# Loading, the first block and the last denominators of an attention kernel rearranged

## The chip, the cores and the metric

The kernel runs on one core of a Trainium2 chip. The metric is the device time of one execution in microseconds (us); where several runs are shown, their median counts. A core has five engines that each work off their own list of instructions in order: TensorE (PE in the profile; its weight loads are PEld), VectorE (DVE), ScalarE (ACT), GpSimd (POOL) and SyncE (SP), which here issues nearly all transfers. Engines wait for each other by semaphores.

## The reference

A layer norm of `x` (2048 x 512, bf16) feeds two branches, which are added to `x`:

```
xn  = layernorm(x)
qkv = xn @ wqkv                       # 32 heads of 16
p   = softmax(q k^T / 4)              # 2048 x 2048 for each head
A   = (p v) @ wo
h   = layernorm(xn)
B   = (gelu(h^T w1 + b1) w2 + b2)^T   # mixes tokens: w1 is 2048x1376
out = x + A + B
```

The exponentials, 32 x 2048 x 2048 of them, are the bulk of the elementwise work.

## The kernel before, in words

**Tiling.** The 2048 tokens are 16 tiles of 128. The attention runs over 32 blocks: for each of four blocks of 512 queries, eight sets of four heads, of which the four live in 32-row strips of TensorE. A block has 16 groups, one for each tile of 128 keys, so there are 512 groups. The scores of a group are four matmuls of 32 x 128 by 512 queries (`score_mm`, L553).

**Two ways to the exponential.** A group goes either to ScalarE, as two exponentials of 128 x 1024 from a pair of PSUM banks (`exp_tile`, L561; banks 0 and 1, or 2 and 3), or to VectorE, which builds it from integer arithmetic on the bits of bf16: four instructions from PSUM (L607) and two further "planes" in SBUF (L612). The products with V (L573) are added up in bank 6 (`PV_BANK`). V has a 17th column of ones for each head, so row 16 of each strip of bank 6 holds the denominator of the softmax. A second copy of V, `V17b`, is scaled by 0.75 for the third plane. The columns of zeros and ones between the heads are written by `v_consts`.

**Order.** The program is written out by a planner in Python. `sc.add` appends an instruction to an engine's list and gives it a planned start from `occ` (how long it holds the engine) and `lat` (until its result can be read); `dma` does the same for transfers. These durations decide only the order. The beginning is an order by hand: loads, constants, statistics and normalization of the first four tiles (`ln_stats1`, `ln_stats2`, `ln_norm`), their transposes (`transpose_mm`) and evacuations (`xnT_evac`), K of the first four tiles and the first 512 queries (`k_mm`, `qt0_mm`, `k_evac`, `qt_evac`). `zeros(n)` puts n matmuls with zero weights on TensorE in between. From there a dispatcher takes engine by engine: it places scores for the next free pair of banks, fills TensorE with products, projections and the MLP's matmuls as far as they end within `TOL` of the next scores, hands groups to VectorE when that has little left to do, and adds a zero matmul (L1524) where TensorE had fewer than `KEEP` units of work in the last 3.4 us. Tiles 4 to 15 go through the chains `ln1` (statistics, normalization), `tp` (transpose) and `kv` (K and V for the first four heads) while block 0 is already running.

**The end.** In each block but the last the denominators travel through DRAM to be inverted and spread. In the last one, `tail_epilogue`, VectorE spreads row 16 of each strip over 32 rows by a shuffle of 128 x 256 (two halves), ScalarE forms exp(-ln(d)), and VectorE multiplies; then come a matmul with the second half of the last rows of `wo` for each of four output tiles (`op_half`, L906), the addition of the rest (`fin`, L1702) and the store.

Of the kernel before, what the change touches and what calls it, by code (L numbers as in the profile page):

```python
# [8 lines left out]
ACTF = mybir.ActivationFunctionType  # L9
# [248 lines left out]
def bass_parallel_sum__softmax_full_mha__mixer_token_mlp__prompt_kernel(  # L258
# [18 lines left out]
    with ExitStack() as es:  # L277
# [67 lines left out]
        def dma(q, dst, src, reads, writes, name="", noncontig=False, out_dma=False, lat=2500.0, move=150.0):  # L345
# [4 lines left out]
            else:  # L350
                def fn(eng, dst=dst, src=src):
# [9 lines left out]

        sc.add("pool", lambda e: e.memset(ident[:], 0.0), writes=[("ident",)], occ=300)
        sc.add("pool", lambda e: e.affine_select(ident[:], ident[:], [[-1, 128]], ALU.not_equal, 1.0,
                                                 base=0, channel_multiplier=1),
               reads=[("ident",)], writes=[("ident",)], occ=600)
        sc.add("pool", lambda e: e.memset(mhalf[:], -0.5), writes=[("mhalf",)], occ=200)
        v17_views = []
# [16 lines left out]
        sc.add("pool", lambda e: e.memset(qmask[:, 0:1], 0.0), writes=[("qmask",)], occ=200)  # L384
        for r in range(4):
            sc.add("pool", lambda e, r=r: e.memset(qmask[32 * r:32 * r + 16, 0:1], QSCALE),
                   reads=[("qmask",)], writes=[("qmask",)], occ=200)
        sc.add("pool", lambda e: e.tensor_scalar(qmask[:, 1:2], qmask[:, 0:1], -1.0, QSCALE, ALU.mult, ALU.add),
               reads=[("qmask",)], writes=[("qmask",)], occ=250)

# [118 lines left out]

        def qt_evac(qb, T, e_, bk, eng="dve"):  # L510
            slot = (8 * qb + 2 * T + e_) % NQS
            if eng == "act":
                return sc.add("act", lambda e: e.activation(QT[:, slot, :], bank(bk), ACTF.Identity,
                                                            scale=qmask[:, e_:e_ + 1]),
                              reads=[("bank", bk), ("qmask",)], writes=[("QT", slot)], occ=560, lat=740)
            return sc.add("dve", lambda e: e.tensor_scalar(QT[:, slot, :], bank(bk), qmask[:, e_:e_ + 1], None,
                                                           ALU.mult),
                          reads=[("bank", bk), ("qmask",)], writes=[("QT", slot)], occ=650, lat=790)

# [30 lines left out]
        def score_mm(g, r, bk, last):  # L550
            b, kt, qb, G, T, e_ = blk_of(g)
            slot_q = b % NQS
            return sc.add("pe", lambda e: e.matmul(  # L553
                bank(bk), lhsT=KT[32 * r:32 * r + 32, T, 128 * kt:128 * (kt + 1)],
                rhs=QT[32 * r:32 * r + 32, slot_q, :], start=True, stop=True,
                tile_position=(32 * r, 0)),
                reads=[("KTt", T, kt), ("QT", slot_q), ("QTr", slot_q, r)], writes=[("bank", bk)], name="sc",
                occ=(222.0 if last else 4.0), lat=430.0, cfg="S")
# [94 lines left out]
        def xnT_evac(t, n, bk, half, eng):  # L653
            dst = xnT[:, t // 4, :, 128 * (t % 4):128 * (t % 4 + n)].rearrange("p c (n j) -> p n c j", n=n)
            src = ps_bf[:, bk * 1024 + half * 512: bk * 1024 + (half + n) * 512].rearrange(
                "p (n c j) -> p n c j", n=n, c=NCT)
            if n == 1:
                dst, src = dst[:, 0], src[:, 0]
            return evac(eng, dst, src, reads=[("bank", bk)], writes=[("xnT", t + i) for i in range(n)], n=256 * n)

# [39 lines left out]
        qt_evac(0, 0, 1, QB, "dve")  # L700
        v_consts(0, "pool")


# [274 lines left out]
        def chain_ln1(t, due):  # L978
            def fin():
                op = ln_norm(t)  # L980
                ln1_done.add(t)
                return op
            return Chain("ln1.%d" % t, [Step("dve", lambda: ln_stats1(t), 755),
                                        Step("pool", lambda: ln_stats2(t), 820),
                                        Step("dve", fin, 300, two=True)], due, 0.0)

# [377 lines left out]
        def pv_candidates(t):  # L1364
            b = pv_block[0]
            if b >= NBLK or not pv_open[0]:
                return []
            return [it for it in pv_items[b] if it[0] <= t and (b > 0 or it[2] % NKT in (v0_done if it[1] == "A" else v0b_done))]

# [20 lines left out]

        TOL = 120.0
        JOIN = 45.0
# [65 lines left out]
        def pe_step(t):  # L1458
# [78 lines left out]

        KEEP = 8.0
        n_zero = [0]

# [129 lines left out]
        def tail_epilogue():  # L1670
            b = NBLK - 1
            po = par_o(b)

            sc.add("act", lambda e: e.activation(u_sb[:, 0:1], r2[:, 0:1], ACTF.Ln), reads=[("r2",)], writes=[("u",)],
                   occ=2800)
            HC = 256
            halves = [slice(HC * i, HC * (i + 1)) for i in range(2)]

            def spread(i):
                sc.add("dve", lambda e: e.stream_shuffle(denb[:, halves[i]], bank(PV_BANK)[:, halves[i]], [16] * 32),  # L1680
                       reads=[("bank", PV_BANK)], writes=[("denb", r) for r in range(4)] if i == 0 else [("denc", 1)],
                       occ=360, lat=490)

            def invert(i):
                key = ("denb", 0) if i == 0 else ("denc", 1)
                for f, sl in ((ACTF.Ln, 1.0), (ACTF.Exp, -1.0)):
                    sc.add("act", lambda e, f=f, sl=sl: e.activation(denb[:, halves[i]], denb[:, halves[i]], f, scale=sl),  # L1687
                           reads=[key], writes=[key], occ=64 + HC / 1.2, lat=242 + HC / 1.2)

            def mult(i):  # L1690
                key = ("denb", 0) if i == 0 else ("denc", 1)
                sc.add("dve", lambda e: e.tensor_tensor(otmp[:, po, halves[i]], bank(PV_BANK)[:, halves[i]],
                                                        denb[:, halves[i]], ALU.mult),
                       reads=[("bank", PV_BANK), key], writes=[("otmp", po, 2 * i), ("otmp", po, 2 * i + 1)],
                       **T_DVE(HC))
                for c in (2 * i, 2 * i + 1):
                    op_half(1, 1, c, c, False, True)
# [102 lines left out]
```

## Time and profile before

| | us |
|---|---|
| median of three runs | 709.04 (708.06 to 709.98) |
| the profiled execution | 710.63 |
| its span, first to last instruction | 708.8 |
| ScalarE busy | 690.5 (97%) |
| VectorE busy | 666.1 (94%) |
| TensorE busy | 655.9 (93%) |
| GpSimd busy | 62.9 (9%) |
| first exponential of ScalarE starts | 11.42 |
| last exponential of ScalarE starts | 694.1 |

A line of a group or of the timeline reads: line of the kernel, engine, operation, what is written from what, shapes and count. In the list of groups the busy time follows and the mean of one in ns, then the idle time of the engine just ahead of them and what ended it. In the timeline the first two numbers are the start and the length in us. In tables by stretch the first number is the stretch's length, and each engine's busy time has its count of instructions behind it. A busy TensorE is not TensorE at its peak: each matmul of 512 columns is recorded with some 0.39 us, while a row of them starts one every 0.22.

### The profile page before, as it was taken

How to read it: one execution, taken by the hardware profiler on the slowest of the kernel's cores; microseconds unless marked ns; L12 is line 12 of the kernel's file. 1: busy time of each engine (PE TensorE's matmuls, PEld its weight loads, DVE VectorE, ACT ScalarE, POOL GpSimd, SP SyncE). 2: the span in 40 equal slices, each digit the busy share in tenths (PEclk: the TensorE clock that was granted, in tenths of full speed). 3: DMA queues.
4: the chain of work that ended last, by engine and by line, in shares of the span. 5: the costliest groups of instructions: out<-in, count | busy, mean ns of one | idle time of the engine just before them, and what ended most of it. 6: DMA issues, size and time to landing. Idle time of an engine off the chain costs nothing.

```text
span 708.8 us, 15538 instructions
## 1 busy us (share of the span) xinstructions
PE 655.9 (93%) x6146; PEld 201.3 (28%) x6235; DVE 666.1 (94%) x1152; ACT 690.5 (97%) x760; POOL 62.9 (9%) x91
## 2 busy tenths in 40 slices
PE   8999999999999999999999999998999999898984
PEld 4533333222222222222222222222222222222221
DVE  6889999999999999999999999999999999999994
ACT  5899999999999999999999999999999999999996
POOL 6420100000000000000000000000000000000000
PEclk9899999999999999999999999999999999999998
DMA  7015110122230312002221212211211111111000
GB/s 208 1 47 101 34 27 4 27 47 55 53 73 15 75 46 53 17 20 54 59 56 47 68 38 48 52 44 44 56 45 38 40 35 54 25 30 31 17 30 30
DMA packets 78368, 32.66 MB, mean 46 GB/s; under 512 B 63004, under 2 KB 74204, under 8 KB 78296
## 3 DMA queue, kind: packets, MB, share of 16 engines
q1 hardware_dynamic: 77240, 31.40, 18.3%
q8 instruction: 49, 0.80, 0.5%
q10 hardware_dynamic: 1056, 0.26, 0.2%
q14 instruction: 23, 0.19, 0.1%
HBM read 26.08 MB, written 2.61 MB: 40 GB/s over the span
## 4 chain that ended last, share of the span: by engine, by line
ACT 88%; PE 8%; DVE 3%; issue 1%; DMA 0%; DVEq 0%; ACTq 0%; SPq 0%
ACT pT L561 86%; PE ps L553 3%; PE ps L573 3%; PE ps L493 1%; DVE x_sb L607 1%; ACT ga_sb L872 1%; PE ps L626 1%; ACT L1687 1%; PE ps L888 0%; DMA x_sb<-in_A_x_dram 0%; PE ps L898 0%; DVE plx L607 0%; DVE stats L442 0%; DVE x_sb L612 0%; DVE xn_sb L612 0%
## 5 line engine op out<-in xcount | busy, mean ns | idle before, releaser
L561 ACT ACTIVATE pT<-ps 128x1024 bf16<-128x1024 f32 x734 | 676.3, 1131 | 4.8 <-PE ps L553 4.6
L553 PE MATMUL ps<-QT,KT 32*128 32x512 bf16 x2048 | 291.7, 385 | 28.6 <-ACT pT L561 23.7
L607 DVE TENSOR_SCALAR x_sb<-ps 128x512 int16<-128x512 f32 x404 | 274.9, 685 | 14.2 <-PE ps L553 1.2
L553 PEld LDWEIGHTS ps<-QT,KT 32*128 32x128 bf16 x2048 | 74.3, 91 | 284.6 <-ACT pT L561 271.6
L573 PE MATMUL ps<-pT,V 128*32 128x512 bf16 x1468 | 146.1, 392 | 2.4 <-DVE V L489 0.8
L607 DVE TENSOR_SCALAR plx<-ps 128x512 int16<-128x512 f32 x148 | 98.4, 682 | 1.3 <-PE ps L553 0.8
L612 DVE TENSOR_SCALAR x_sb<-x_sb 128x2048 int16<-128x2048 int16 x135 | 92.8, 693 | 3.3 <-PE ps L573 2.7
L573 PE MATMUL ps<-x_sb,V 128*32 128x512 bf16 x812 | 77.0, 382 | 1.3 <-DVE x_sb L612 1.0
L573 PEld LDWEIGHTS ps<-pT,V 128*32 128x32 bf16 x1468 | 37.3, 93 | 83.8 <-issue 74.5
L888 PE MATMUL ps<-gT,w2blk 128*128 128x512 bf16 (+1 forms) x148 | 49.3, 385 | 3.0 <-issue 2.5
L851 PE MATMUL ps<-h_sb,w1blk 128*128 128x512 bf16 (+1 forms) x154 | 48.7, 385 | 2.1 <-issue 1.9
L1104 POOL TENSOR_TENSOR oT<-OT,denb 128x512 bf16<-128x512 f32 x16 | 20.4, 1272 | 324.6 <-DVE x_sb L612 175.8
L1104 POOL TENSOR_TENSOR otmp<-OT,denb 128x512 bf16<-128x512 f32 x15 | 19.1, 1272 | 280.9 <-DVE x_sb L612 155.3
L612 DVE TENSOR_SCALAR x_sb<-plx 128x2048 int16<-128x2048 int16 x62 | 42.1, 685 | 0.2
L573 PE MATMUL ps<-x_sb,V17b 128*32 128x512 bf16 x416 | 40.8, 382 | 0.2 <-DVE x_sb L612 0.2
L493 PE MATMUL ps<-xnT,wqkv_sb 128*128 128x512 bf16 (+1 forms) x166 | 35.0, 309 | 3.3 <-issue 2.6
L612 DVE TENSOR_SCALAR plx<-x_sb 128x2048 int16<-128x2048 int16 x48 | 33.1, 689 | 1.0 <-PE ps L573 0.5
L573 PE MATMUL ps<-plx,V 128*32 128x512 bf16 x284 | 27.7, 381 | 0.7 <-DVE OT L1067 0.6
L573 PEld LDWEIGHTS ps<-x_sb,V 128*32 128x32 bf16 x812 | 21.8, 96 | 16.1 <-issue 7.5
L1067 DVE COPY OT<-ps 128x512 f32<-128x512 f32 x31 | 21.1, 680 | 0.1
L493 PE MATMUL ps<-wqkv_sb,xnT 128*128 128x128 bf16 x256 | 21.1, 223 | 0.0
L888 PEld LDWEIGHTS ps<-gT,w2blk 128*128 128x128 bf16 (+1 forms) x176 | 12.8, 97 | 26.9 <-issue 22.9
(88 smaller groups left out, 358.6 us busy)
## 6 DMA issues: line engine op xcount, KB each, us to landing
denb<-rec_scr SPq DMA_DIRECT2D x124, 64.0 KB, 2.1
w1blk<-in_B_w_dram SPq DMA_DIRECT2D x10, 512.0 KB, 4.3
w2blk<-in_B_w_dram SPq DMA_DIRECT2D x16, 320.0 KB, 3.4
xres<-in_A_x_dram SPq DMA_DIRECT2D x16, 128.0 KB, 2.4
QT<-qst SPq DMA_DIRECT2D x120, 16.0 KB, 1.8
out_dram<-osb SPq DMA_DIRECT2D x14, 128.0 KB, 1.7
wqkv_sb<-in_A_wqkv_dram SPq DMA_DIRECT2D x3, 384.0 KB, 7.4
x_sb<-in_A_x_dram SPq DMA_DIRECT2D x2, 512.0 KB, 6.3
```

Source lines behind the costliest of these rows:

```text
L493: return sc.add("pe", lambda e: e.matmul(dst, lhsT=lhsT, rhs=rhs, start=(ct == 0), stop=(ct == NCT - 1)), reads=reads, writes=[("bank", bk ...
L553: return sc.add("pe", lambda e: e.matmul(bank(bk), lhsT=KT[32 * r:32 * r + 32, T, 128 * kt:128 * (kt + 1)], rhs=QT[32 * r:32 * r + 32, slo ...
L561: return sc.add("act", lambda e: e.activation(pT[:, buf, :], ps[:, slot * 1024:(slot + 1) * 1024], ACTF.Exp, scale=EXP_SCALE), reads=[("ba ...
L573: return sc.add("pe", lambda e: e.matmul(bank(PV_BANK)[32 * r:32 * r + 32, :], lhsT=vt_[:, off:off + 32], rhs=rhs, start=start, stop=stop, ...
L607: return sc.add("dve", lambda e: e.tensor_scalar(plane_i[pb][:, 512 * r:512 * (r + 1)], bank(bk), BIAS, 0.0, ALU.add, ALU.max), reads=[("b ...
L612: return sc.add("dve", lambda e: e.tensor_scalar(plane_i[pb], plane_i[pb0], float(SHIFT[j]), BITS_MAX, ALU.add, ALU.min), reads=[("pl", pb ...
L626: op = sc.add("pe", lambda e, ct=ct: e.transpose(ps_bf[:, bk * 1024 + half * 512 + ct * 128: bk * 1024 + half * 512 + (ct + 1) * 128], xn_ ...
L851: op = sc.add("pe", lambda e: e.matmul(bank(xb)[0:m, :], lhsT=w1blk[:, slot, st, 0:m], rhs=h_sb[:, st, :], start=(st == 0), stop=(st == NT ...
L872: steps.append(Step("act", lambda: sc.add("act", lambda e: e.activation(ga_sb[0:m, :], ga_sb[0:m, :], ACTF.Tanh, scale=2.0 * GELU_C), read ...
L888: op = sc.add("pe", lambda e: e.matmul(bank(xb), lhsT=w2blk[0:m, slot, ft, :], rhs=gT[0:m, ft, :], start=first, stop=last), reads=([("w2bl ...
L1067: op = sc.add("dve", lambda e: e.tensor_copy(OT32[:, eb, :], bank(PV_BANK)), reads=[("bank", PV_BANK)], writes=[("OT32", eb)], **T_DVE(512))
L1104: op = sc.add("pool", lambda e: e.tensor_tensor(dst, OT32[:, eb, :], denb[:, :], ALU.mult), reads=[("OT32", eb)] + [("denb", r) for r in r ...
```

## The change

- The way from the last products to the last denominators is replaced. Each half of bank 6 (128 x 256) is transposed in 32 x 32 blocks by VectorE, which brings a strip's 16 rows of output and its denominator into the columns of one row; eight reciprocals are formed for each partition, 8 x 16 products, and a second transpose of 32 x 32 blocks brings them back. The shuffles, ScalarE's Ln and Exp and the early Ln are gone.
- In the beginning the first K block and the first query product come ahead of tile 1's transpose; tile 2's evacuation is on ScalarE and tile 3's on VectorE; tile 3's epsilon is added on VectorE. The queries of tile 3 go to bank 4 and the other three tiles' to bank 7, and each query slot is evacuated in two pieces of 384 and 128 columns, all on ScalarE. Tile 4's statistics join the part written by hand.
- The constants of V move to the start, the ones among them from GpSimd to VectorE; those of `V17b` wait until all tiles are normalized.
- In the first 25 us (planned) zero matmuls are added up to 12 units instead of 8; `TOL` is 140 instead of 120; products of block 0 are picked only when the planner holds V ready.
- The planner's durations for constants and first loads are changed; the order in which the loads are issued is the same.

```diff
 def v_consts(i, eng):
...
-                sc.add(eng, lambda e: e.memset(main[:, :, 16:17], 1.0), writes=[("Vone",)], occ=2000)
+                sc.add("dve", lambda e: e.memset(main[:, :, 16:17], 1.0), writes=[("Vone",)], occ=620)
...
+        v_consts(0, "pool")
...
         for t in range(NPRE):
-            ld_x(t, t + 1, 2500)
-        ld_w(1, 0, 1, 3500)
-        ld_w(0, 0, 1, 3800)
+            ld_x(t, t + 1, 2150 + 60 * t)
+        ld_w(1, 0, 1, 2900)
+        ld_w(0, 0, 1, 3000)
...
         def ln_stats2(t):
-            sc.add("pool", lambda e: e.tensor_scalar(mv[:, t, 3:4], mv[:, t, 1:2], EPS, None, ALU.add),
-                   reads=[("mv", t)], writes=[("mve", t)], occ=300, lat=380)
+            if t == NPRE - 1:
+                sc.add("dve", lambda e: e.tensor_scalar(mv[:, t, 3:4], mv[:, t, 1:2], EPS, None, ALU.add),
+                       reads=[("mv", t)], writes=[("mve", t)], occ=75, lat=210)
+            else:
...
         zeros(6)
         ln_stats(2)
         ln_stats(3)
+        k_mm(0, KB, 0)
+        qt0_mm(0, QB)
+        zeros(1)
         ln_norm(1)
         transpose_mm(1, 5, 0)
+        ln_norm(2)
         xnT_evac(1, 1, 5, 0, "act")
-        k_mm(0, KB, 0)
-        qt0_mm(0, QB)
-        ln_norm(2)
+        k_evac(0, 1, KB, 0)
         transpose_mm(2, 0, 0)
         ln_norm(3)
-        xnT_evac(2, 1, 0, 0, "dve")
+        xnT_evac(2, 1, 0, 0, "act")
+        transpose_mm(3, 1, 0)
+        xnT_evac(3, 1, 1, 0, "dve")
         qt0_mm(1, QB)
-        transpose_mm(3, 1, 0)
-        xnT_evac(3, 1, 1, 0, "act")
-        k_evac(0, 1, KB, 0)
         k_mm(1, 3, 0)
         qt0_mm(2, QB)
-        zeros(1)
-        qt0_mm(3, QB)
-        qt_evac(0, 0, 0, QB, "act")
+        ln_stats(NPRE)
+        qt0_mm(3, 4)
+        qt_evac(0, QB, "act", 0, 384)
+        qt_evac(0, 4, "act", 384, 512, "QTh")
         k_mm(2, 3, 1)
         k_mm(3, 3, 2)
-        zeros(1)
+        qt_evac(1, 4, "act", 384, 512, "QTh")
+        qt_evac(1, QB, "act", 0, 384)
         k_evac(1, 3, 3, 0)
-        qt_evac(0, 0, 1, QB, "dve")
-        v_consts(0, "pool")
...
-        bg.append(Chain("vb", [Step("pool", lambda: v_consts(1, "pool"))], -1.0, 0.0))
+        bg.append(Chain("vb", [Step("pool", lambda: v_consts(1, "pool"), gate=lambda: len(ln1_done) == NT)], -1.0, 0.0))
...
-        TOL = 120.0
+        TOL = 140.0
...
-                if u < KEEP and t + 226.0 + (SWITCH if sc.cfg != "F" else 0.0) <= lim:
+                if u < (KEEP0 if t < T_KEEP0 else KEEP) and t + 226.0 + (SWITCH if sc.cfg != "F" else 0.0) <= lim:
...
+        KEEP0, T_KEEP0 = 12.0, 25000.0
...
+            NB = HC // 32
+
+            def half(i):
+                hs = slice(HC * i, HC * (i + 1))
+                rc = den_s[:, 0, NB * i:NB * (i + 1)]
+                dn = denb[:, hs].rearrange("p (c m) -> p c m", m=32)
+                wt = gT[:, 0, hs].rearrange("p (c m) -> p c m", m=32)
+                dk, rk, wk = ("denb", i), ("den_s", 2 + i), ("gTw", i)
+                sc.add("dve", lambda e: e.transpose(denb[:, hs], bank(PV_BANK)[:, hs]),
+                       reads=[("bank", PV_BANK)], writes=[dk] + ([("denb", r) for r in range(4)] if i == 0 else []),
                        **T_DVE(HC))
+                sc.add("dve", lambda e: e.reciprocal(rc, dn[:, :, 16]), reads=[dk, ("den_s", 0)], writes=[rk], occ=160, lat=290)
+                sc.add("dve", lambda e: e.tensor_tensor(wt[:, :, 0:16], dn[:, :, 0:16],
+                                                        rc.rearrange("p (c o) -> p c o", o=1).broadcast_to([128, NB, 16]),
+                                                        ALU.mult),
+                       reads=[dk, rk], writes=[wk, ("gT", 0)], **T_DVE(HC // 2))
+                sc.add("dve", lambda e: e.transpose(otmp[:, po, hs], gT[:, 0, hs]), reads=[wk, ("gT", 0)],
+                       writes=[("otmp", po, 2 * i), ("otmp", po, 2 * i + 1)], **T_DVE(HC))
                 for c in (2 * i, 2 * i + 1):
                     op_half(1, 1, c, c, False, True)
...
-            spread(0)
-            invert(0)
-            spread(1)
-            invert(1)
-            mult(0)
-            mult(1)
+            half(0)
+            half(1)
             for c in range(4):
                 fin(c)
```

More of the change, by code (lines that the diff above doesn't have):

```diff
@@ L359, in bass_parallel_sum__softmax_full_mha__mixer_token_mlp__prompt_kernel @@
         NPRE = 4
-        sc.add("pool", lambda e: e.memset(ident[:], 0.0), writes=[("ident",)], occ=300)
+        sc.add("pool", lambda e: e.memset(ident[:], 0.0), writes=[("ident",)], occ=200, lat=430)
         sc.add("pool", lambda e: e.affine_select(ident[:], ident[:], [[-1, 128]], ALU.not_equal, 1.0,
                                                  base=0, channel_multiplier=1),
-               reads=[("ident",)], writes=[("ident",)], occ=600)
-        sc.add("pool", lambda e: e.memset(mhalf[:], -0.5), writes=[("mhalf",)], occ=200)
+               reads=[("ident",)], writes=[("ident",)], occ=270, lat=400)
+        sc.add("pool", lambda e: e.memset(mhalf[:], -0.5), writes=[("mhalf",)], occ=60, lat=130)
         v17_views = []
@@ L379, in v_consts @@
             if i == 0:
-                sc.add(eng, lambda e: e.memset(main[:, :, 16:17], 1.0), writes=[("Vone",)], occ=2000)
+                sc.add("dve", lambda e: e.memset(main[:, :, 16:17], 1.0), writes=[("Vone",)], occ=620)
         sc.add("dve", lambda e: e.memset(zw[:], 0.0), writes=[("zw",)], occ=80)
         sc.add("dve", lambda e: e.memset(KT[:, 1, 0:512], 0.0), writes=[("KTt", 1, t) for t in range(4)], occ=200)
-        sc.add("pool", lambda e: e.memset(qmask[:, 0:1], 0.0), writes=[("qmask",)], occ=200)
+        sc.add("pool", lambda e: e.memset(qmask[:, 0:1], 0.0), writes=[("qmask",)], occ=130, lat=140)
         for r in range(4):
             sc.add("pool", lambda e, r=r: e.memset(qmask[32 * r:32 * r + 16, 0:1], QSCALE),
-                   reads=[("qmask",)], writes=[("qmask",)], occ=200)
+                   reads=[("qmask",)], writes=[("qmask",)], occ=135, lat=145)
         sc.add("pool", lambda e: e.tensor_scalar(qmask[:, 1:2], qmask[:, 0:1], -1.0, QSCALE, ALU.mult, ALU.add),
-               reads=[("qmask",)], writes=[("qmask",)], occ=250)
+               reads=[("qmask",)], writes=[("qmask",)], occ=190, lat=260)
+        v_consts(0, "pool")
         def ld_x(a, b_, lat):
@@ L447, in ln_stats2 @@
         def ln_stats2(t):
-            sc.add("pool", lambda e: e.tensor_scalar(mv[:, t, 3:4], mv[:, t, 1:2], EPS, None, ALU.add),
-                   reads=[("mv", t)], writes=[("mve", t)], occ=300, lat=380)
+            if t == NPRE - 1:
+                sc.add("dve", lambda e: e.tensor_scalar(mv[:, t, 3:4], mv[:, t, 1:2], EPS, None, ALU.add),
+                       reads=[("mv", t)], writes=[("mve", t)], occ=75, lat=210)
+            else:
+                sc.add("pool", lambda e: e.tensor_scalar(mv[:, t, 3:4], mv[:, t, 1:2], EPS, None, ALU.add),
+                       reads=[("mv", t)], writes=[("mve", t)], occ=300, lat=380)
             return sc.add("pool", lambda e: e.tensor_tensor(mv[:, t, 2:3], mv[:, t, 3:4], mhalf[:, 0:1], ALU.pow),
@@ L508, in qt_mm, with qt_evac @@
                            [("wqkv", 0, T)] + [("xnT", t) for t in range(4 * qb, 4 * qb + 4)], bk)
-        def qt_evac(qb, T, e_, bk, eng="dve"):
-            slot = (8 * qb + 2 * T + e_) % NQS
+        def qt_evac(slot, bk, eng, a=0, b=512, key="QT"):
+            dst, src = QT[:, slot, a:b], bank(bk)[:, a:b]
             if eng == "act":
[L513 to L518, printed above, removed]
+                return sc.add("act", lambda e: e.activation(dst, src, ACTF.Identity, scale=qmask[:, slot:slot + 1]),
+                              reads=[("bank", bk), ("qmask",)], writes=[(key, slot)], occ=64 + (b - a) / 1.2,
+                              lat=242 + (b - a) / 1.2)
+            return sc.add("dve", lambda e: e.tensor_scalar(dst, src, qmask[:, slot:slot + 1], None, ALU.mult),
+                          reads=[("bank", bk), ("qmask",)], writes=[(key, slot)], **T_DVE(b - a))
         def v_mm(t, T, j, bk):
@@ L556, in score_mm @@
                 tile_position=(32 * r, 0)),
-                reads=[("KTt", T, kt), ("QT", slot_q), ("QTr", slot_q, r)], writes=[("bank", bk)], name="sc",
+                reads=[("KTt", T, kt), ("QT", slot_q), ("QTr", slot_q, r)] + ([("QTh", b)] if b < 2 else []), writes=[("bank", bk)], name="sc",
                 occ=(222.0 if last else 4.0), lat=430.0, cfg="S")
@@ L658, in xnT_evac @@
                 dst, src = dst[:, 0], src[:, 0]
-            return evac(eng, dst, src, reads=[("bank", bk)], writes=[("xnT", t + i) for i in range(n)], n=256 * n)
+            return evac(eng, dst, src, reads=[("bank", bk)], writes=[("xnT", t + i) for i in range(n)],
+                        n=(450 if eng == "act" else 256) * n)
         QB, KB, VB = EX_BANK, PV_BANK, 2
@@ L982, in fin @@
                 return op
-            return Chain("ln1.%d" % t, [Step("dve", lambda: ln_stats1(t), 755),
-                                        Step("pool", lambda: ln_stats2(t), 820),
-                                        Step("dve", fin, 300, two=True)], due, 0.0)
+            steps = [Step("dve", lambda: ln_stats1(t), 755), Step("pool", lambda: ln_stats2(t), 820)]
+            return Chain("ln1.%d" % t, (steps if t > NPRE else []) + [Step("dve", fin, 300, two=True)], due, 0.0)
         def chain_tp(t, due):
@@ L1367, in pv_candidates, with v_ready @@
                 return []
-            return [it for it in pv_items[b] if it[0] <= t and (b > 0 or it[2] % NKT in (v0_done if it[1] == "A" else v0b_done))]
+            return [it for it in pv_items[b] if it[0] <= t and (
+                b > 0 or (it[2] % NKT in (v0_done if it[1] == "A" else v0b_done) and v_ready(it) <= t))]
+        def v_ready(it):
+            which = 0 if it[1] == "A" or WEIGHT[it[4]] == 1.0 else 1
+            return sc.ready(reads=[("V", which, it[2] % NKT, 0), ("Vone",), ("Vpad", which)])
         def pv_issue(it):
@@ L1672, in tail_epilogue @@
             po = par_o(b)
-            sc.add("act", lambda e: e.activation(u_sb[:, 0:1], r2[:, 0:1], ACTF.Ln), reads=[("r2",)], writes=[("u",)],
-                   occ=2800)
             HC = 256
[L1677 to L1694, printed above, removed]
-                       **T_DVE(HC))
+            NB = HC // 32
```

## The prediction

> **What bounds the kernel now.** I read the page's chain and groups first, then the order in time of ScalarE, then TensorE's clock by stretches, then the last 14 us.
>
> ```profile
> PEclk9899999999999999999999999999999999999998
> ACT 88%; PE 8%; DVE 3%; issue 1%; DMA 0%; DVEq 0%; ACTq 0%; SPq 0%
> L561 ACT ACTIVATE pT<-ps 128x1024 bf16<-128x1024 f32 x734 | 676.3, 1131 | 4.8 <-PE ps L553 4.6
> PEld ps L553 <- ACT pT L561: 271.6, 669, 0.9
> ```
>
> ScalarE is the bound: 734 exponentials, which follow each other every 0.917 us (124 of them in 113.77 us of the chain). In front of them it idles 4.8 us in all, nearly always for scores (L553). Those in turn normally wait for ScalarE to free their banks, 0.4 us on average in 669 cases: TensorE is early. ScalarE's order in time, columns start and length:
>
> ```profile
> 10.16 0.69 ACT L513 ACTIVATE QT<-ps,qmask 128x512 bf16<-128x512 f32 x1 [0.49 <-PE ps L493]
> 11.42 5.61 ACT L561 ACTIVATE pT<-ps 128x1024 bf16<-128x1024 f32 x6 [0.57 <-PE ps L553]
> 17.18 1.02 ACT L561 ACTIVATE pT<-ps 128x1024 bf16<-128x1024 f32 x1 [0.16 <-PE ps L553]
> 18.82 1.02 ACT L561 ACTIVATE pT<-ps 128x1024 bf16<-128x1024 f32 x1 [0.61 <-PE ps L553]
> 22.57 20.49 ACT L561 ACTIVATE pT<-ps 128x1024 bf16<-128x1024 f32 x22 [2.73 <-PE ps L553]
> ```
>
> At its pace the ninth exponential would start at 11.42 + 8 x 0.917 = 18.76; it starts at 22.57, 3.8 us late. The reader sees why in the stretches (the number behind POOL's is the granted TensorE clock):
>
> ```profile
> 12.10:15.50 3.40, 2.51 (x23) 0.90 (x19) 3.30 (x10) 3.40 (x5) 1.80 (x6) 1.00 0.68 134
> 15.50:18.90 3.40, 3.40 (x25) 1.63 (x24) 2.96 (x8) 2.63 (x4) 1.59 (x5) 0.51 0.00 0
> 18.90:22.30 3.40, 3.40 (x32) 2.10 (x30) 2.32 (x6) 0.94 (x1) 1.51 (x4) 0.50 0.00 0
> 22.30:25.70 3.40, 2.85 (x36) 1.76 (x33) 2.71 (x8) 3.13 (x4) 0.79 (x2) 0.99 0.00 0
> ```
>
> After a thin stretch (2.51 us busy) the clock is halved for 6.8 us, TensorE is full, and K tiles 4 and 5 with their scores come late. At the other end everything hangs on the last block's denominators:
>
> ```profile
> 697.67 0.44 DVE L1680 STREAM_SHUFFLE denb<-ps 128x256 f32<-128x256 f32 x1
> ...
> 698.14 0.42 ACT L1687 ACTIVATE denb<-denb 128x256 f32<-128x256 f32 x1 [1.44 <-DVE denb L1680]
> ...
> 698.57 1.28 ACT L1687 ACT_TABLE_LOAD   x1
> ...
> 700.30 1.28 ACT L1687 ACT_TABLE_LOAD   x1
> ...
> 702.03 1.28 ACT L1687 ACT_TABLE_LOAD   x1
> ...
> 703.77 0.42 DVE L1692 TENSOR_TENSOR otmp<-ps,denb 128x256 bf16<-128x256 f32 x1 [3.03 <-ACT denb L1687]
> ```
>
> From the shuffle to the end of the second multiplication it takes 6.52 us (697.67 to 704.19), of which three table loads on ScalarE are 3.84.
>
> **The tail.** All of this lies on the path. Each half becomes four dependent VectorE instructions. A transpose of 128x256 has no row; nearest is the shuffle of the same size from the same bank, 0.44, and as ends 0.43 (the multiplication's row) and 0.88 (twice the shuffle, if four-byte elements take two passes). I take the shuffle's, for both transposes. The reciprocal of 8 columns: that of 16 has 0.24, the shortest VectorE arithmetic of the start 0.17; I take 0.24. The product of 128 columns: the cast of that size 0.28, at most the multiplication's 0.43. Dependent neighbours start 0.03 apart (statistics to aggregate, 11.74 + 0.69 to 12.46). A half is 0.44 + 0.24 + 0.28 + 0.44 + 4 x 0.03 = 1.52, both 3.04; gain 6.52 - 3.04 = 3.5, between 1.4 (0.88 for each transpose, 0.43 for the product) and 3.7. What follows (matmuls, four additions, stores, 4.6 us) stays. The removed Ln ahead of it (695.20 to 696.70) lay beside the last products and is worth nothing.
>
> The row is three loads around four activations. By the Trainium skill (ScalarE: Activation LUTs, "Table sets: the hidden batching unit") one set holds ln and exp, so that the pair needs one load. By that the old chain would be 6.52 - 3.84 = 2.68 and the new one 0.4 longer; this trace does load three times, and the trace decides.
>
> **Up to the first exponential.** The loads' issue order is not changed: only the durations that the planner believes are. Their queues (x on SP, two weights on ScalarE's) stay, so nothing is gained there. The first block of K and the first query product move ahead of tile 1's transpose: they need the transposed tile 0 (6.45) and weights whose queue is empty by 4.5; they run behind the six zeros, about 6.95, then one zero, so transpose 1 slips from 7.33 to about 7.65. Tile 3's epsilon moves to VectorE: POOL then starts its power behind tile 2's, near 7.2 instead of 7.43, but tile 0's K copy (0.28) now sits ahead of tile 3's normalization, which comes at about 7.95 (8.04 before). Tile 3's transpose follows near 8.4, its copy goes to VectorE (0.42 instead of ScalarE's 0.60), queries near 9.4 to 9.8. In place of one evacuation of 512 columns (0.69) behind them, only 128 columns wait: 0.31 to 0.42 (the 256-column activation is 0.42). The other query slot, 0.74 on VectorE before, adds about 0.6 on ScalarE ahead of the first exponential, covered by the scores' 0.39 plus 0.1; a remainder of 0.1 is included. I get 10.9 for 11.42: 0.5, between 0.2 and 0.8.
>
> **Constants.** POOL's first memsets (0.81 + 0.11) move before its first wait (3.86, idle 1.43 there); the ones (2.27 on POOL) move to VectorE's idle 1.64 ahead of 2.87, at about 0.6 by POOL's 0.27 for 256 columns. Both cost nothing; were VectorE's cover gone, 0.6. The second set (1.24) is held until the last normalization; behind it on POOL stands only the clearing of query slots, and its readers, third planes of block 0, start after 41 in this trace. Nothing, or 1.2 of POOL time without that cover.
>
> **The first block.** Tile 4's statistics (0.69 + 0.18) fit VectorE's idle 1.55 ahead of 10.61, and the query evacuation (0.74) leaves it. K tiles 4 and 5 should be copied near 16.5 (20.63 before), wanted by about 17.8. Zeros, of which the trace has one between 11 and 60 us, are now added up to 12 units instead of 8 in the first 25 us. Each takes about 0.22 (six in 1.46) where TensorE would wait for banks. The bounds: they keep the clock and all 3.8 us return, or none; below nothing, four of them each holding a score back by 0.22 would cost 0.9. I take the upper end less what is next late: K pairs come 3.9 us apart (20.21 to 39.79 in five steps) where ScalarE eats one in 3.67, so the fifth pair costs about 0.7. Gain 3.1.
>
> **The rest.** 20 ns more tolerance and other start times make the planner deal the groups anew. One group moved between ScalarE and VectorE is two exponentials, 1.8 us: taken as zero, between -1.8 and +1.8.
>
> **Sum.** 0.5 + 3.1 + 3.5 = 7.1. The profiled execution took 710.63 (span 708.8 and 1.8 around it): 703.5. It stands 1.6 above the median of the runs shown, 709.04, so for that median 701.9.
>
> **Rivals.**
> - The zeros do not hold the clock. For it: with full clock the thin stretch has only two or three places per exponential for a zero. Against: at 2.85 us busy (22.3 to 25.7) it held. Earlier K still returns 1.0: 709.04 - 0.5 - 1.0 - 3.5 = 704.0. Chance 0.14.
> - The half-clock stretch is a matter of where the kernel starts within the gate's steps, and the median runs mostly lacked it: then it returns nothing, 705.0. For it: all three runs lie below the profiled one; against: by 1.6 us, not 3.8. Chance 0.10. The Trainium skill (TensorE: Matmul & The Clock Gate, "The HAM clock gate") has a window of some 3.4 us that runs free of the kernel; the trace's 6.8 us is two of them.
> - VectorE becomes the bound of block 0: it was busy 3.30 of 3.40 us at 12 to 15.5, and 2 us of the stall stay: 703.2. Chance 0.10.
> - One group goes back to ScalarE: 703.7, chance 0.07; one leaves it: 700.1, chance 0.05.
> - The transposes cost 0.88: 704.0, chance 0.02.
> - Slower: the tolerance of 140 ns lets fill work stand in front of scores. If each of 734 came 20 ns later at ScalarE, 14.7 us less 7.1: 716.6. It decides only where the margin is used up; a score takes 0.39 and the other bank pair's exponential 0.917, so some 0.4 us are spare, save where TensorE is late (434 to 445, 0.53 us lost). Chance 0.05.
>
> **How the numbers follow.** The forecast has 0.41; two or more of the losses together, ending within 0.3% (2.1 us, about what a measurement here tells from nothing), 0.06. Faster is 0.41 + 0.14 + 0.10 + 0.10 + 0.07 + 0.05 + 0.02 = 0.89. The range goes down to 699.8 (0.8 at the start, all 3.8, 3.7 in the tail and half a group) and up to 705.8 (the 705.0 case and half a group), leaving about 0.14 out.
>
> **What would show it.** The first exponential near 10.9; granted clock 1.00 from 8 to 26 and ScalarE's idle there under 1 us; no table load after the last exponential, and about 3.0 us from the first transpose to the end of the last; 734 exponentials, give or take two. The prediction is wrong if the clock still falls, if the count of exponentials moves by four or more, or if the last product waits for VectorE's planes long after ScalarE has ended (2.4 us now).

## The result and the profile after

The changed kernel takes 704.00 us (703.88 to 704.77), beside 708.55 (707.23 to 710.26) for the one before: a ratio of 0.9935, 95% interval 0.9919 to 0.9951. The profiled execution took 704.31 with a span of 702.5, 6.3 less than the profiled one of before; the medians lie only 4.55 apart, and 3.8 against the 707.8 of the later comparisons. That gap between profile and median is half of the story below.

From the page of the changed kernel:

```profile
PEclk9999999999999999999999999999999999999999
L566 ACT ACTIVATE pT<-ps 128x1024 bf16<-128x1024 f32 x734 | 676.5, 1125 | 2.1 <-PE ps L558 1.9
```

ScalarE still has 734 exponentials and is still the bound (82% of the page's chain); the clock does not fall in this execution. Its order in time (start, length; the last column is the idle time in front):

```profile
10.01 1.56 ACT L519 ACTIVATE QT<-ps,qmask 128x384 bf16<-128x384 f32 x4 [0.49 <-PE ps L499]
11.45 7.45 ACT L566 ACTIVATE pT<-ps 128x1024 bf16<-128x1024 f32 x8
19.41 9.27 ACT L566 ACTIVATE pT<-ps 128x1024 bf16<-128x1024 f32 x10 [0.51 <-PE ps L558]
29.43 11.22 ACT L566 ACTIVATE pT<-ps 128x1024 bf16<-128x1024 f32 x12 [0.75 <-PE ps L558]
```

The first exponential is not earlier in this execution (11.45, 11.42 before), the gap of 3.8 us ahead of the ninth has shrunk to 0.5, and a new one of 0.75 stands ahead of the nineteenth. The tail, VectorE's part:

```profile
694.90 0.45 DVE L1695 STREAM_TRANSPOSE denb<-ps 128x256 f32<-128x256 f32 x1 [0.65 <-PE ps L578]
695.39 0.20 DVE L1698 RECIPROCAL den_s<-denb 128x8 f32<-128x8 f32 x1
695.63 0.29 DVE L1699 TENSOR_TENSOR gT<-denb,den_s 128x128 bf16<-128x128 f32 x1
695.95 0.45 DVE L1703 STREAM_TRANSPOSE otmp<-gT 128x256 bf16<-128x256 bf16 x1
...
697.33 0.45 DVE L1703 STREAM_TRANSPOSE otmp<-gT 128x256 bf16<-128x256 bf16 x1
697.80 1.29 DVE L1711 TENSOR_TENSOR osb<-ps,h_sb 128x512 bf16<-128x512 f32 x2
```

The old chain ended ahead of this addition in the profile of before:

```profile
704.12 1.28 DVE L1702 TENSOR_TENSOR osb<-ps,h_sb 128x512 bf16<-128x512 f32 x2
```

From the first transpose to the first addition it is now 2.90; from the shuffle at 697.67 to the addition at 704.12 it was 6.45. Gain: 3.55.

### The profile page after: what moved, and what is told of

It reads as the page before. It is cut to its first block, busy times and chain, and to the rows that moved or that the text cites. A ratio compares the mean times of both kernels' runs of the same rounds, so it can differ in the third digit from the quotient of the medians.

```text
span 702.5 us, 15631 instructions
## 1 busy us (share of the span) xinstructions
PE 670.9 (95%) x6238; PEld 200.8 (29%) x6238; DVE 665.5 (95%) x1155; ACT 684.5 (97%) x754; POOL 61.0 (9%) x89
## 4 chain that ended last, share of the span: by engine, by line
ACT 82%; PE 12%; DVE 4%; issue 1%; DMA 0%; DVEq 0%; SPq 0%
ACT pT L566 81%; PE ps L578 4%; PE ps L558 4%; DVE x_sb L612 2%; PE ps L895 2%; PE ps L905 1%; ACT ga_sb L879 1%; DVE plx L612 1%; PE ps L499 1%; DMA x_sb<-in_A_x_dram 0%; DVE x_sb L617 0%; DVE OT L1073 0%; PE ps L631 0%; PE ps L671 0%; DVE plx L617 0%
## 5 line engine op out<-in xcount | busy, mean ns | idle before, releaser
L612 DVE TENSOR_SCALAR x_sb<-ps 128x512 int16<-128x512 f32 x404 | 274.2, 683 | 15.6 <-PE ps L558 2.5
L612 DVE TENSOR_SCALAR plx<-ps 128x512 int16<-128x512 f32 x140 | 92.6, 680 | 1.9 <-PE ps L558 1.6
L617 DVE TENSOR_SCALAR x_sb<-x_sb 128x2048 int16<-128x2048 int16 x130 | 88.7, 684 | 1.9 <-PE ps L578 1.2
L895 PE MATMUL ps<-gT,w2blk 128*128 128x512 bf16 (+1 forms) x176 | 57.1, 386 | 0.3 <-DVE h_sb L972 0.2
L858 PE MATMUL ps<-h_sb,w1blk 128*128 128x512 bf16 (+1 forms) x176 | 54.0, 386 | 0.3 <-DVE plx L612 0.2
L499 PE MATMUL ps<-xnT,wqkv_sb 128*128 128x512 bf16 (+1 forms) x188 | 40.6, 315 | 1.6 <-DVE xnT L495 0.7
L617 DVE TENSOR_SCALAR plx<-x_sb 128x2048 int16<-128x2048 int16 x46 | 31.5, 685 | 1.5 <-PE ps L578 1.5
L578 PE MATMUL ps<-plx,V 128*32 128x512 bf16 x264 | 26.0, 381 | 0.2 <-DVE plx L617 0.2
L612 DVE TENSOR_SCALAR xn_sb<-ps 128x512 int16<-128x512 f32 x36 | 24.6, 683 | 1.6
```

Source lines behind the costliest of these rows:

```text
L499: return sc.add("pe", lambda e: e.matmul(dst, lhsT=lhsT, rhs=rhs, start=(ct == 0), stop=(ct == NCT - 1)), reads=reads, writes=[("bank", bk ...
L578: return sc.add("pe", lambda e: e.matmul(bank(PV_BANK)[32 * r:32 * r + 32, :], lhsT=vt_[:, off:off + 32], rhs=rhs, start=start, stop=stop, ...
L612: return sc.add("dve", lambda e: e.tensor_scalar(plane_i[pb][:, 512 * r:512 * (r + 1)], bank(bk), BIAS, 0.0, ALU.add, ALU.max), reads=[("b ...
L617: return sc.add("dve", lambda e: e.tensor_scalar(plane_i[pb], plane_i[pb0], float(SHIFT[j]), BITS_MAX, ALU.add, ALU.min), reads=[("pl", pb ...
L858: op = sc.add("pe", lambda e: e.matmul(bank(xb)[0:m, :], lhsT=w1blk[:, slot, st, 0:m], rhs=h_sb[:, st, :], start=(st == 0), stop=(st == NT ...
L895: op = sc.add("pe", lambda e: e.matmul(bank(xb), lhsT=w2blk[0:m, slot, ft, :], rhs=gT[0:m, ft, :], start=first, stop=last), reads=([("w2bl ...
```

## The experiments

My theory after the result: the tail gives nearly everything, and the first block's 3.1 us were counted from an execution that most do not resemble. The rival: the start gives its part, and the tail less.

**The two halves of the change, and its zeros.**

Tail only (the kernel before, with the new tail):

```diff
-            spread(0)
-            invert(0)
...
+            half(0)
+            half(1)
```

> The kernel before with the new tail alone; the rest of its instructions is unchanged. If the tail's gain simply adds (old chain 6.52 us, new chain 2.90 from the first transpose at 694.90 to the first addition at 697.80 in the changed kernel), this kernel takes 3.6 us less than the one before, about 705.0, and nearly the whole measured gain of 4.5 is the tail's. Rival: the start does most of it, and the tail gains under 1.5: above 707.

Measured: 704.51, ratio 0.9947 (0.9930 to 0.9964) against 707.8 in 23 runs of the kernel before: 3.3 less. The chain from first transpose to first addition is 2.80 (697.02 to 699.82).

Start only (the changed kernel with the old tail):

```diff
-            half(0)
-            half(1)
+            spread(0)
+            invert(0)
...
```

> The changed kernel with the old tail (shuffle, Ln, Exp, multiplication). If the tail's 3.6 add, this takes 704.0 + 3.6 = 707.6, so that everything else together is worth about 1 us. Rival: the two profiles are right that 2.7 us come from outside the tail (6.3 less 3.6): about 705.9.

Measured: 708.01, ratio 0.9995 (0.9984 to 1.0006). All of the change but its tail is worth nothing that can be measured; putting the new tail to it takes 4.0 away. The theory holds. The early Ln was rightly costed at nothing, though its cover is thin in this run's profile: ScalarE was done with it at 696.44, only 0.34 before the first activation that needs a shuffle's result (696.78).

The kernel before with more zeros only:

```diff
-                if u < KEEP and t + 226.0 + (SWITCH if sc.cfg != "F" else 0.0) <= lim:
+                if u < (KEEP0 if t < T_KEEP0 else KEEP) and t + 226.0 + (SWITCH if sc.cfg != "F" else 0.0) <= lim:
...
+        KEEP0, T_KEEP0 = 12.0, 25000.0
```

> The kernel before with 12 units instead of 8 in the first 25 us and nothing else; the planned order has three zeros after the first products instead of one. If the thin stretch at 12 to 15.5 us makes the clock fall, it now holds: clock 1.00 up to 26, ScalarE idle under 1.5 us between 11 and 38, and 2 to 3 us less than before, about 706. Rival: the fall is a matter of the phase of one execution, median runs mostly lack it: within 0.7 of 708.5.

Measured: 707.40, ratio 0.9989 (0.9980 to 0.9999). The profile shows the forecast clock of 1.00 up to 26 us, but neither expectation has the time: it is 1.1 below the 708.5 around which the rival's band of 0.7 was laid, but only 0.4 below the 707.8 of the runs it was compared with. All twelve runs lie between 707.1 and 708.0, while of the 23 of the kernel before 8 lie between 709.5 and 710.2 (the upper group) and the rest between 707.3 and 708.1. So with the old start the zeros take away the upper group and hardly move the lower one.

The changed kernel with fewer zeros:

```diff
-        KEEP0, T_KEEP0 = 12.0, 25000.0
+        KEEP0, T_KEEP0 = 8.0, 25000.0
```

> The changed kernel with 8 units instead of 12 in the first 25 us: one zero in place of three. If the zeros hold the clock, it falls here to about 0.5 near 15 to 22 and the kernel takes 1 to 3 us more than 704.0. Rival: the earlier work on tiles 4 and 5, not the zeros, made the stretch dense enough: within 0.5 of 704.0.

Measured: 704.05 (704.03 to 704.39), ratio 0.9942 (0.9928 to 0.9956); the clock stayed at 1.00 from 8.7 to 40 us in the profile. The first theory, that the zeros alone hold it here, is not borne out. Six runs of which none is longer than 704.4 are not proof that this kernel has no upper group: at the old kernel's 8 of 23 one would get six such by chance about one time in thirteen, and at the 16 of 59 counted below about one time in seven.

**What the upper group is.** The kernel before was profiled once more, unchanged.

> The kernel before, unchanged, for a second profile. Its 23 runs so far fall into 15 of 707.3 to 708.1 and 8 of 709.6 to 710.1. If the upper group is the executions whose clock falls in the first block, this look shows either about 707.5, a clock of 1.00 throughout 12 to 26 us and ScalarE idle there near 1.1 (as with the two more zeros), or about 709.9 with the fall again. Rival: 707.5 with the fall in place, and the two groups come from elsewhere.

Measured: 708.05, span 706.3. Its stretches (the number behind POOL's is the granted clock) and ScalarE's order:

```profile
12.10:15.50 3.40, 2.51 (x24) 1.00 (x21) 3.29 (x10) 3.40 (x5) 1.90 (x7) 1.00 0.82 177
15.50:18.90 3.40, 3.31 (x42) 2.08 (x40) 3.33 (x9) 3.40 (x4) 1.85 (x6) 1.00 0.00 0
18.90:22.30 3.40, 3.12 (x42) 1.79 (x40) 3.33 (x11) 2.29 (x4) 1.50 (x4) 1.00 0.00 0
```

```profile
11.51 7.44 ACT L561 ACTIVATE pT<-ps 128x1024 bf16<-128x1024 f32 x8 [0.57 <-PE ps L553]
20.06 20.49 ACT L561 ACTIVATE pT<-ps 128x1024 bf16<-128x1024 f32 x22 [1.11 <-PE ps L553]
```

The stretch at 12.1 to 15.5 is as thin as in the first profile, 2.51 us busy, and yet the clock does not fall; ScalarE loses 1.11, not 3.5. The tail-only kernel has the start of the kernel before, and its profiled execution was the slowest of its six (706.28). It shows the fall again, in this stretch and the next:

```profile
15.50:18.90 3.40, 3.40 (x25) 1.68 (x24) 2.96 (x8) 2.64 (x4) 1.63 (x5) 0.50 0.00 0
```

The same program thus meets the clock in two ways. The fall costs some 2.3 us: ScalarE waits 3.50 instead of 1.11 for the ninth exponential and the two before it, and the two groups of the 23 runs lie 2.3 apart in the mean. The mean clock on record for each run goes with the groups: 0.990 or 0.991 in the eight of the upper one, 0.995 to 0.997 in the others. That difference, some 0.005 of 708 us, is 3.5 us, about what 6.8 us at half clock lose (3.4). Over all 59 runs of the kernel before, 16 lie at 709.4 or above, two at 709.0 and 41 at 708.2 or below.

The clock records kept in the traces (`prof` shows them only as means over a window, with 1.00 ahead of the first) tell more. In the first profile and in the tail-only one the full clock begins 5.32 and 5.26 us after the span's start, and the half clock 10.24 later, at 15.56 and 15.50, for 6.83: three and two steps of 3.41. Counted in such steps, the thin stretch fills one step whole (12.14 to 15.56, TensorE 2.53 busy). In the second profile of before the full clock begins at 4.51; the thin stretch is then divided between two steps (11.33 to 14.75, 2.67 busy, and 14.75 to 18.16, 3.18 busy), and nothing falls. So where the steps lie in an execution fits the difference. The Trainium skill (TensorE: Matmul & The Clock Gate, "The HAM clock gate") says that the gate's window runs free of the kernel; these two profiles of one kernel agree. The busy time of a step alone does not decide, though: the changed kernel has one with 2.47 (593.32 to 596.73) and keeps its clock.

From the first exponential to the first instruction of the tail's chain the profiles give, worked out from their rows (the last line is a kernel described further below):

| kernel | first exponential | from there to the chain | clock falls |
|---|---|---|---|
| before | 11.42 | 686.25 | at 15.6 |
| tail only | 11.37 | 685.65 | at 15.5 |
| start only | 11.29 | 685.02 | at 596.5 |
| before, again | 11.51 | 683.61 | no |
| zeros only | 11.23 | 682.88 | no |
| changed | 11.45 | 683.45 | no |
| changed, fewer zeros | 11.05 | 683.58 | no |
| before, new tail and zeros | 11.77 | 683.19 | no |

With the clock up, the rearranged start gains nothing on this way: what it saves ahead of the ninth exponential it loses again at the nineteenth (0.75) and at 373 us (0.60).

Nor does the rearranged start, with its zeros, end the falls. The start-only kernel's profile (709.29, the longest of its twelve) has the clock at 1.00 from 8.7 to 40 us, and at half from 596.5 to 599.9, after a step with TensorE 2.46 of 3.41 us busy:

```profile
598.39 1.02 ACT L566 ACTIVATE pT<-ps 128x1024 bf16<-128x1024 f32 x1 [0.70 <-PE ps L558]
```

ScalarE waits 0.70 there and 0.50 once more, 1.2 us in all. A fall in the first block is thus one place among others.

**Is the rest of the start worth anything?** The kernel before with the new tail and the zeros, and nothing else.

```diff
+        KEEP0, T_KEEP0 = 12.0, 25000.0
...
+            half(0)
+            half(1)
```

> The kernel before with the new tail and with 12 units in the first 25 us, and nothing else of the change: the old order of the start, old constants, tolerance 120. If the start's rearrangement is worth nothing once the clock holds, this takes 707.4 - 3.55 = 703.8, the changed kernel's 704.0 within 0.4, with no executions 2 us above. Rival: the rearrangement is worth the half microsecond or more that was forecast: 704.5 or above.

Measured: 703.52 (703.28 to 704.21), ratio 0.9939 (0.9926 to 0.9953). These two parts do all that the whole change does, with an interval that overlaps it; the new order of the start, the constants, the tolerance and the bank for the last tile's queries together add nothing on top that these runs can tell.

**Why the first exponential came no earlier.**

```diff
-        k_mm(0, KB, 0)
-        qt0_mm(0, QB)
-        zeros(1)
         ln_norm(1)
         transpose_mm(1, 5, 0)
+        k_mm(0, KB, 0)
+        qt0_mm(0, QB)
+        zeros(1)
...
-        qt_evac(1, 4, "act", 384, 512, "QTh")
-        qt_evac(1, QB, "act", 0, 384)
+        qt_evac(1, 4, "dve", 384, 512, "QTh")
+        qt_evac(1, QB, "dve", 0, 384)
```

> The changed kernel with tile 1's transpose put back ahead of the first K block and the first query product, and with the second query slot evacuated by VectorE again. If tile 1's slip behind the zeros (transpose at 8.01, 7.33 before) and the four evacuations on ScalarE are what ate the expected half microsecond, the first exponential comes at 10.7 to 10.9 instead of 11.45, and the time falls by up to 0.6 to 703.4. Rival: K tile 4 is the next bound, the ninth exponential stays near 19.4, and the time stays at 704.0.

Measured: 705.87, ratio 0.9973 (0.9962 to 0.9985): 1.9 longer than the changed kernel. The first exponential came at 11.60, which neither expectation had. Two things mix here. The six early zeros (5.89) took 2.12 us, because the clock rose late in that execution: its clock records begin at 7.21, and with those of 4.2 to 5.3 in other profiles the same six take 1.46. And VectorE's query pieces (11.22, 0.88) stood ahead of the K copy out of bank 3 (12.01), which takes the second exponential's scores; that exponential waited 0.42 for them, and later ones 0.64 and 0.47. The run with both edits, further below, separates the two in part. Kernels that share a start show the first of them better (full clock from 4.2 to 5.3 in the first line, 6.0 to 6.2 in the second, 6.7 to 7.2 in the third):

| early zeros take | old start, first exponential | new start |
|---|---|---|
| 1.46 | 11.23, 11.37, 11.42, 11.51 | 11.03, 11.05 |
| 1.55 to 1.65 | | 11.29, 11.38, 11.45 |
| 1.80 to 2.25 | 11.75, 11.77 | 11.90 |

With the clock up in time the new start is 0.34 earlier (11.38 to 11.04 in the mean), from six profiles of which the old start's four lie 0.28 apart; a late clock takes more than that away.

**The tail further.** First the three instructions on all 512 columns at once:

```diff
-                sc.add("dve", lambda e: e.transpose(denb[:, hs], bank(PV_BANK)[:, hs]),
...
+            sc.add("dve", lambda e: e.transpose(denb[:, :], bank(PV_BANK)[:, :]),
...
```

> The changed kernel with the tail's first three instructions over all 512 columns instead of two halves; the second transpose stays in halves. The eight instructions took 2.90 us from the first transpose to the first addition. If each has a fixed part of about 0.15 us besides its columns, five instructions take 0.72 + 0.27 + 0.43 + 2 x 0.40 = 2.2: 0.65 less, 703.4. Rival: the columns alone count (about 0.34 per 256), or the matmuls of the first half, which now start later, take the gain back: within 0.2 of 704.0.

Measured: 704.63, ratio 0.9957 (0.9942 to 0.9972): no gain. Its timeline (TensorE's and VectorE's rows) tells why:

```profile
695.49 0.72 DVE L1692 STREAM_TRANSPOSE denb<-ps 128x512 f32<-128x512 f32 x1 [0.65 <-PE ps L578]
...
696.99 0.77 DVE L1702 STREAM_TRANSPOSE otmp<-gT 128x256 bf16<-128x256 bf16 x2
697.10 0.81 PE L905 MATMUL ps<-wo_c,oT 128*128 128x512 bf16 x3
...
697.97 1.03 PE L913 MATMUL ps<-wo_pad,otmp 128*128 128x512 bf16 x4
698.38 1.29 DVE L1710 TENSOR_TENSOR osb<-ps,h_sb 128x512 bf16<-128x512 f32 x2 [0.62 <-PE ps L913]
```

VectorE's five instructions take 2.27 (695.49 to 697.76), but TensorE has its prepared products in front and reaches the first of the last products at 697.97. The first addition comes 2.89 after the first transpose, as before. TensorE is what is late next.

The whole tail together with the start of the run before (tile 1's transpose first) was expected at 702.8 if both added, or at 703.4 if the start gave nothing. Measured: 705.56 (704.63 to 706.94, ten runs), ratio 0.9959 (0.9947 to 0.9972), 0.9 longer than the whole tail alone: that start loses. In its profile the six early zeros took 1.46, so the clock was up in time, and the first exponential still came at 11.29, with the same waits of 0.42, 0.64 and 0.47 behind it. Of the 0.56 between 11.60 and the new start's 11.04, one profile each, 0.31 thus goes with the late clock and 0.25 with the order. This profile (706.71) also has a fall far from the start, at half clock from 199.1 to 202.5.

With the changed start as it was, TensorE's products for the last tile were then put behind:

```diff
                 for c in (2 * i, 2 * i + 1):
+                    if c == 3:
+                        for T in range(3):
+                            op_mm(3, c, T, c, T == 0, False)
+                        op_half(1, 0, c, c, False, False)
                     op_half(1, 1, c, c, False, True)
```

> The changed kernel with the whole tail, and with TensorE's four products for the last output tile placed behind the last halves of the first three. With the whole tail alone VectorE's five instructions took 2.27 us, but TensorE worked until 698.1 on the sixteen products in front, and the first addition started 2.89 after the first transpose, as before. If TensorE's list is the bound there, the first addition now starts about 2.4 after the first transpose and the time falls by 0.4 to 0.5, to about 703.5 to 703.6. Rival: the last tile's products then delay the fourth addition by as much: 704.0.

```profile
694.61 0.72 DVE L1692 STREAM_TRANSPOSE denb<-ps 128x512 f32<-128x512 f32 x1 [0.65 <-PE ps L578]
...
697.04 1.29 DVE L1714 TENSOR_TENSOR osb<-ps,h_sb 128x512 bf16<-128x512 f32 x2 [0.16 <-PE ps L913]
```

The chain is 2.43 now, as the theory asked. The time is 703.74 (703.53 to 705.32), ratio 0.9947 (0.9931 to 0.9964): the 0.47 are in the profile, but in the medians only 0.3 of them against 704.0, less than these runs can tell. The same tail and split on the kernel before with the added zeros:

> The kernel before with the zeros of the first 25 us, the whole tail and the split of TensorE's last products; the start otherwise as before. If the tail's parts add and the start does not matter, 0.45 under the kernel with the half-wise tail and zeros: about 703.3. Rival: no gain from the split, 703.8.

Measured: 703.69 (703.50 to 703.87), ratio 0.9941 (0.9928 to 0.9953), no better than 703.52 for the same start with the tail in halves, as its rival had it. Its profile has the chain at 2.43 as well, with a first exponential at 11.75: the start's scatter is as large as what is left to gain here.

**The tolerance.**

```diff
-        TOL = 140.0
+        TOL = 120.0
```

> The changed kernel with the tolerance back at 120 ns. The planner then gives VectorE one group more: 732 exponentials on ScalarE instead of 734. If a group is worth its 1.83 us on ScalarE, 702.2; rival: VectorE, 95% busy, ends as much later, or TensorE's stretches bind, and the time stays within 0.7 of 704.0 or is longer.

Measured: 708.34, ratio 1.0007 (0.9997 to 1.0016): 4.3 longer than the changed kernel. ScalarE has 732 exponentials and ends at 692.0, 1.5 earlier, but VectorE is still at its planes:

```profile
697.24 0.69 DVE L617 TENSOR_SCALAR plx<-xn_sb 128x2048 int16<-128x2048 int16 x1 [0.22 <-PE ps L578]
699.04 0.45 DVE L1695 STREAM_TRANSPOSE denb<-ps 128x256 f32<-128x256 f32 x1 [0.51 <-PE ps L578]
```

The tail starts 7.0 us after ScalarE's last exponential, 1.4 in the changed kernel. In this deal one group more for VectorE is a loss of 4, not a gain of 1.8. That this comes from the tolerance itself was not shown: it acts through the whole deal of groups, and with the old start the kernels at 120 have 734 exponentials.

## Why the prediction was right, and where it was not

The range and the sign held: 704.0 within 699.8 to 705.8. The forecast of 701.9 was 2.1 too low, and the sum fails mainly in one term. That the range held owes something to luck: it was laid from 709.04, the median of three runs, and 23 later runs of that kernel have 707.8. Against these the gain is 3.8, little over half of the 7.1 forecast. Two rivals named 704.0 as well, that the zeros do not hold the clock and that transposes cost 0.88; neither happened in the changed kernel's profile.

- **Tail, 3.5: right.** The chain was forecast at 3.04 to the end of the last transpose and measured at 2.88, 2.90 to the first addition; the gain is 3.55. Transposes cost 0.41 to 0.45, near the shuffle's 0.44, in both types; the reciprocal 0.20 for 0.24, the product 0.29 for 0.28. The Trainium skill (VectorE: DVE Perf Modes, "The three transpose paths") has 311 ns for 128x128 bf16; with 128 further columns at the 1.05 ns that each costs between the 0.45 of 256 columns and the 0.72 of 512 here, that is an estimate of 0.45, and the trace agrees. That the old chain with its three table loads was on the path fits the two halves of the change: the tail-only kernel has none of them and gains 3.3, the start-only kernel still has them and gains nothing.
- **First block, 3.1: wrong.** The failing step is "I take the upper end less what is late next", on bounds read from a single execution. There the 3.8 us were real, but by their times most executions do not have the fall: with the clock up the same kernel loses 1.11, the changed one 0.51 and 0.75. On the way to the tail's chain the start is then worth nothing (683.45 beside 683.61), and the start-only kernel gains nothing (708.01 beside 707.8). The rival "a matter of where the kernel starts within the gate's steps", given 0.10 and 705.0, is what these profiles show. The argument against it, that the runs lay only 1.6 under the profiled execution, was the wrong reading: the runs had two groups 2.3 apart, and three of them could not show it. The sum even takes a gain worked out on the execution of 710.63 off a median 1.6 below it. And the sign named beforehand, a clock of 1.00 from 8 to 26, came true, but most executions of the kernel before have it too.
- **First exponential, 0.5: half right.** At equal clock it is 0.34, within 0.2 to 0.8; it is then lost again. In the profile it was nothing (11.45), as tile 1's transpose slipped to 8.01 rather than 7.65: the zeros began 0.21 later than before (5.86) and took 1.65 instead of 1.46.
- **K tiles 4 and 5** were copied at 18.32, not 16.5: TensorE's K products for them (16.20 and 17.43) stand among scores that wait for ScalarE, and the copy comes behind 0.69 + 0.18 of statistics on VectorE. The rival in which VectorE bounds block 0 was thus partly right: it is busy 3.31 to 3.37 of 3.40 us between 15.5 and 25.7.
- **Zeros:** no sign that they cost anything. Their worth is the upper group that is missing with the old start; that they hold the clock in the changed start is not shown, as it held with fewer, and falls at other places remain.
- **The deal of groups, 0 between -1.8 and +1.8:** zero held, as both kernels have 734 exponentials, but the bounds were too narrow: one group cost 4.3 in the tolerance experiment. A group moved to VectorE was priced as if VectorE, 94% busy, had room; in that run VectorE's last plane ends 4.3 later than in the changed kernel.
- **The slower rival** (140 ns delays scores) did not come: ScalarE's exponentials waited 1.9 us for scores in all.

## What to carry to other kernels

A stall that hangs on a granted clock should be looked for in a second execution before it is priced: here the profile showed one that, by their times, 15 of 23 runs did not have. A chain of small dependent steps at the end of a kernel could be priced here from rows of neighbouring shapes to 0.2 us, but once it is shortened the next engine's list (here TensorE's prepared products) sets the end. Where a planner balances two engines, ask what the engine that receives a piece makes of it: here that set the price.

## What the runs showed of the hardware

A stretch with TensorE busy 2.51 of 3.40 us was followed by half clock in two profiles and by full clock in another of the same instructions. All falls ahead of the tail lasted 3.41 or 6.83 us, and they began a whole number of 3.41 us steps after the clock's rise. The rise itself came between 4.2 and 7.2 us after the span's start: the same six zero matmuls took 1.46 to 2.25 us, and with the new start the first exponential moved with it from 11.03 to 11.90. A VectorE transpose of 128x256 takes 0.41 to 0.45 from four-byte and 0.45 from two-byte elements, and one of 128x512 four-byte elements 0.72.
